# Attention scores in sixteen 32 by 32 tiles instead of four 32 by 128 tiles, and the memory write by the heads of each tile

## The chip, the cores and the metric

One core of one Trainium2 chip. The metric is the time of the kernel on the device in microseconds (us). "Clock" is the mean share of full speed that TensorE (PE) was granted.

## The reference, cut to what matters

Two layers run one after the other, twice, over 2048 tokens of 640 features: an attention with a compressive memory (32 heads of 20 features, four segments of 512 tokens), and a feed-forward block of width 1728. In the attention, every segment `s` does:

```python
logits = jnp.einsum('bhqd,bhkd->bhqk', qs, ks) * scale + mask
p = _softmax(logits, axis=-1)
a_dot = jnp.einsum('bhqk,bhkd->bhqd', p, vs)
# ... read of the memory M, z
o = g * a_mem + (1.0 - g) * a_dot
pk = phi(ks)
M = M + jnp.einsum('bhld,bhle->bhde', pk, vs)
z = z + jnp.einsum('bhld->bhd', pk)
```

The change touches two of these products: the logits (called scores here), and the update of `M`, `z` (the memory write).

## The kernel before

A scheduler written in Python simulates the engines, and fixes the order of every engine's instructions before the program is built. It knows three modes of TensorE: "full" (128 by 128), "cols" (four column tiles of 128 by 32) and "rows" (four row tiles of 32 by 128), and charges 96 ns for a change of mode. A dense product may run in full or in column mode; it takes the mode that TensorE is in, and full mode after scores:

```python
def _mode(self, op):
    if op.cols is None:
        return op.mode
    return self.mode if self.mode != "rows" else "full"

# in _alts:
if e == "pe" and self._mode(op) != self.mode:
    hold = hold + SWITCH_NS          # 96.0
```

Scores. A head has 20 features, so four heads lie at partitions 0, 32, 64 and 96, and their matmuls run at once in four row tiles, one wave of four. A block of scores is one or two such waves and always 512 columns of streaming, because the causal mask shortens the later key blocks:

```python
ROUNDS = (((0, 0, 0),), ((0, 1, 0), (0, 3, 384)), ((0, 2, 0), (1, 2, 256)),
          ((1, 0, 0),), ((1, 1, 0), (1, 3, 384)))     # (group, key block j, column offset)
...
for y, (z, j, o) in enumerate(parts):
    N = L - 128 * j
    fns.append([(lambda e, ...: e.matmul(
        slot.ap[:, q, o:o + N], sl.ap[32 * hh:32 * hh + DH, z, 0, 128 * j:128 * j + 128],
        sl.ap[32 * hh:32 * hh + DH, z, 1, 128 * j:L]),
        y == len(parts) - 1 and hh % 2 == 1) for hh in (2 * k, 2 * k + 1)])
...
return pe(221.0, fns, ..., mode="rows"), None
```

There are 160 such blocks. After each, ScalarE takes the exponential, and later TensorE multiplies the probabilities with the values in four column tiles ("cols").

Memory write. 128 features of the keys against the values of all heads that they touch (7 or 8 heads of 21 columns); a mask drops later what belongs to other heads. In column mode each column tile holds 32 features:

```python
def mm(e, b, rows, part, c=c, i=i, ...):
    return e.matmul(
        b.ap[rows, CH_OFF[c] - o0:CH_OFF[c + 1] - o0], part,
        VAUG[vx(a, s)][:, i, CH_H0[c]:CH_H1[c], :].rearrange("p h e -> p (h e)"),
        start=st, stop=True, skip_group_check=True)
```

The softmax here doesn't subtract the row's maximum and nothing guards it: scores larger than these inputs give would overflow.

Of the kernel before, what the change touches and what calls it, by code (L numbers as in the profile page):

```python
# [12 lines left out]
DH = 20  # L13
# [96 lines left out]
class Op:  # L110
# [4 lines left out]
    def __init__(self, alts, waits, dma=None, acq=None, urgent=False, take=(), mode="full", lag=0.0, port=False):  # L115
        self.lag = lag
        self.port = port
        self.alts = alts
        self.mode = mode
        self.cols = None  # L120
        self.acq = acq
        self.waits = [t for t in waits if t is not None]
        self.dma = dma
        self.urgent = urgent
        self.take = take
# [44 lines left out]
class Sched:  # L170
# [63 lines left out]
    def _alts(self, op):  # L234
        res = []
        waits = op.waits
        if op.acq is not None:
            s = self._pick(op.acq)
            if s is None:
                return res  # L240
            waits = waits + s.tks
        for k, (e, hold, fns, tail) in enumerate(op.alts):
            m = PE_MARGIN if e == "pe" else 0.0
            if e == "pe" and self._mode(op) != self.mode:
                hold = hold + SWITCH_NS
            start = max([self.at(t) + SEM_NS + m for t in waits], default=0.0)
            start = max(self.free[e], start)
            if e == "dve" and op.port and self.free["pool"] > start:
                hold = max(hold, self.free["pool"] - start + PORT_NS)
            res.append((start + hold, start, k, e))  # L250
        return res
# [100 lines left out]
    return Op([("pe", ns, fns, 190.0)], waits, acq=acq, take=take, mode=mode, lag=lag)  # L352


def either(op, cols):
    op.cols = cols
    return op


def quarters(a):  # L360
# [34 lines left out]
def bass_interleave_layers__memory_aug_infini_attn__dense_activation_relu__prompt_kernel(  # L395
    nc, A_x, A_wq, A_wk, A_wv, A_wo, A_beta, B_x, B_w1, B_w2, out,
):
    with contextlib.ExitStack() as es:
# [463 lines left out]
        def vx(a, s):  # L862

            return 2 if (a, s) == (0, 0) else s % 2
# [195 lines left out]
        def mem_write(a, s):  # L1060
            mg = yield Need("maskg")
            if s < NSEG - 1:
                vt = yield Need("v", a, s)
                upd = []
                lastd = None
                for p, cs in enumerate(PARTS):
                    pht = yield Need("phkT", a, s, p)
                    o0 = CH_OFF[cs[0]]
                    w = CH_OFF[cs[-1] + 1] - o0
                    bk = None  # L1070
                    for i in range(NJ):
                        fns, cols = [], []
                        for c in cs:
                            def mm(e, b, rows, part, c=c, i=i, o0=o0, st=(i == 0 and c == cs[0])):
                                return e.matmul(  # L1075
                                    b.ap[rows, CH_OFF[c] - o0:CH_OFF[c + 1] - o0], part,
                                    VAUG[vx(a, s)][:, i, CH_H0[c]:CH_H1[c], :].rearrange("p h e -> p (h e)"),
                                    start=st, stop=True, skip_group_check=True)
                            end = i == NJ - 1 and c == cs[-1]
                            fns.append((lambda e, b=None, bk=bk, mm=mm, kt=phk[:, c, i, :]: mm(e, b or bk, slice(0, 128), kt), end))  # L1080
                            for y, (rows, part) in enumerate(quarters(phk[:, c, i, :])):
                                cols.append((lambda e, b=None, bk=bk, mm=mm, rows=rows, part=part: mm(e, b or bk, rows, part),
                                             end and y == 3))
                        if i == 0:
                            bk, lastd = yield either(pe(66.0 * len(cs), fns, pht + vt, acq=MISC), cols)
                        else:
                            lastd = yield either(pe(66.0 * len(cs), fns), cols)
                    if s == 0:
                        tu = yield dve(w, 1, lambda e, bk=bk, o0=o0, w=w: e.tensor_copy(
                            M_sb[:, o0:o0 + w], bk.ap[:, 0:w]), [lastd] + S.events.get(("BD", a - 1, NSEG - 2), []))  # L1090
                    else:
                        tu = yield dve(w, 1, lambda e, bk=bk, o0=o0, w=w: e.tensor_tensor(
                            M_sb[:, o0:o0 + w], M_sb[:, o0:o0 + w], bk.ap[:, 0:w], ALU.add),
                            [lastd] + S.events[("BD", a, s - 1)])
                    bk.release(tu)
                    PHK[p].release(lastd)
                    if p == 1:
                        S.set("dm", a, s, tks=[lastd])
                    else:
                        bd = yield Acq([BDS])  # L1100
                    tb = yield dve(w, 1, lambda e, o0=o0, w=w: e.tensor_tensor(
                        BD[:, o0:o0 + w], M_sb[:, o0:o0 + w], maskg[:, o0:o0 + w], ALU.mult), [tu] + mg + bd.tks)
                    upd.append(tb)
                S.set("BD", a, s, tks=upd)
            else:
                S.set("dm", a, s, tks=[])
# [8 lines left out]
        def scores():  # L1115

            pads = {}
            LEND_FROM, LEND_TO = ("stg", 0, 0, 4, 1), ("sc", NSEG * 0 + G // 2 - 1, 4, 1)

            def half(h, slot):  # L1120

                m, u, k = HALVES[h]
                parts = ROUNDS[u]
                pd = []
                for z in {z for z, _, _ in parts}:
                    n = 2 * m + z
                    a, r = divmod(n, NSEG * G)
                    key = ("pad", a) + divmod(r, G) + ()
                    if key not in S.events:
                        return None  # L1130
                    pads[m] = S.events[key][0]
                    pd = pd + S.events[key][1:]
                sl = pads[m]
                fns = []
                for y, (z, j, o) in enumerate(parts):
                    N = L - 128 * j
                    fns.append([(lambda e, z=z, j=j, hh=hh, N=N, o=o, sl=sl, q=hh % 2: e.matmul(  # L1137
                        slot.ap[:, q, o:o + N], sl.ap[32 * hh:32 * hh + DH, z, 0, 128 * j:128 * j + 128],
                        sl.ap[32 * hh:32 * hh + DH, z, 1, 128 * j:L]),
                        y == len(parts) - 1 and hh % 2 == 1) for hh in (2 * k, 2 * k + 1)])  # L1140
                return slot, pd, fns

            h = 0
            while h < len(HALVES):
                took = []

                def ask(h=h):
                    if LEND_FROM in S.events and LEND_TO not in S.events:
                        for sl in LENT:
                            if sl in MISC and sl.free:  # L1150
                                MISC.remove(sl)
                                Z.tks = Z.tks + sl.tks
                                if not any(x in MISC for x in LENT):
                                    SC.append(Z)
                    elif LEND_TO in S.events and Z in SC and Z.free:
                        SC.remove(Z)
                        for sl in LENT:
                            sl.tks = Z.tks
                            MISC.append(sl)
                    ready = sorted((s for s in SC if s.free), key=lambda s: max([S.at(t) for t in s.tks], default=0.0))  # L1160
                    if len(ready) < 2 or h + 1 >= len(HALVES):
                        return None, None
                    a, b = half(h, ready[0]), half(h + 1, ready[1])
                    if a is None or b is None:
                        return None, None
                    took[:] = ready[:2]
                    fns = []
                    for y in range(max(len(a[2]), len(b[2]))):
                        for z in (a, b):
                            fns += z[2][y] if y < len(z[2]) else []  # L1170
                    return pe(221.0, fns, a[1] + b[1] + a[0].tks + b[0].tks, take=[a[0], b[0]], mode="rows"), None
                tks = yield Either(ask)
                for tk, sl in zip(tks, list(took)):
                    m, u, k = HALVES[h]
                    S.set("sc", m, u, k, tks=[sl, tk])
                    if (u, k) == (4, 1):
                        pads[m].release(tk)
                    h += 1
# [380 lines left out]
```

## Time and profile before

| | before |
|---|---|
| time, median of 2 runs | 559.84 us (558.76 to 560.91) |
| span of the profiled run | 558.0 us, clock 1.00 |
| score matmuls | 1024 in 160 blocks |
| changes of tile shape on TensorE | 339, together 38.5 us of delay |

The prediction below shows the lines that tell what bounds the kernel. Two more are needed for comparison: the groups of the scores on the profile page (columns: line, engine, operation, names, shapes, count; busy us and mean ns of one; idle time of the engine just before them and who ended most of it).

```profile
L1137 PE MATMUL ps<-pad 20*128 20x512 bf16 (+3 forms) x1024 | 63.4, 301 | 1.7 <-DMA pad<-scr 1.0
L1137 PEld LDWEIGHTS ps<-pad 20*128 20x128 bf16 x1024 | 17.8, 92 | 52.5 <-ACT PT L1199 27.9
```

"20*128" is the tile: 20 rows, 128 weight columns. TensorE hardly idles before scores (1.7 us in all). The idle time of the weight loads, 52.5 us, is no idle time of TensorE: in this trace a load starts 134 ns before its matmul (median) where the shape of the tiles stays, but only 4 ns before it where the shape changes, so its engine shows a gap while matmuls still stream.

### The profile page before, as it was taken

How to read it: one execution, taken by the hardware profiler on the slowest of the kernel's cores; microseconds unless marked ns; L12 is line 12 of the kernel's file. 1: busy time of each engine (PE TensorE's matmuls, PEld its weight loads, DVE VectorE, ACT ScalarE, POOL GpSimd, SP SyncE). 2: the span in 40 equal slices, each digit the busy share in tenths (PEclk: the TensorE clock that was granted, in tenths of full speed). 3: DMA queues.
4: the chain of work that ended last, by engine and by line, in shares of the span. 5: the costliest groups of instructions: out<-in, count | busy, mean ns of one | idle time of the engine just before them, and what ended most of it. 6: DMA issues, size and time to landing. Idle time of an engine off the chain costs nothing.

```text
span 558.0 us, 18924 instructions
## 1 busy us (share of the span) xinstructions
PE 548.0 (98%) x8257; PEld 307.8 (55%) x8257; DVE 422.1 (76%) x1077; ACT 400.1 (72%) x499; POOL 193.5 (35%) x302
## 2 busy tenths in 40 slices
PE   8998999999999999999999999999999999999998
PEld 7454554445554555545446545664545654766756
DVE  5967989979999998797777998688987896552102
ACT  5699888888677987787888887369788678223140
POOL 5336344433344444443433443034334343101000
PEclk9999999999999999999999999999999999999999
DMA  8696999855464417356179231772337511434101
GB/s 271 142 226 156 221 192 207 229 72 110 85 152 83 86 30 173 83 71 113 40 166 168 38 67 41 141 177 46 56 82 176 123 33 20 102 64 47 54 2 51
DMA packets 130005, 61.32 MB, mean 110 GB/s; under 512 B 108802, under 2 KB 119810, under 8 KB 129922
## 3 DMA queue, kind: packets, MB, share of 16 engines
q1 hardware_dynamic: 129504, 59.62, 50.0%
q8 instruction: 65, 1.06, 0.8%
q10 hardware_dynamic: 418, 0.49, 0.3%
q14 instruction: 18, 0.15, 0.1%
HBM read 20.57 MB, written 12.85 MB: 60 GB/s over the span
## 4 chain that ended last, share of the span: by engine, by line
PE 89%; DVE 5%; DMA 4%; SPq 1%; ACT 1%; POOL 0%; issue 0%; ACTq 0%; POOLq 0%
PE ps L636 43%; PE ps L639 26%; PE ps L1137 8%; PE ps L1231 6%; DMA otk<-otu 2%; PE ps L1075 1%; PE ps L1018 1%; PE ps L1270 1%; PE ps L616 1%; PE ps L1411 1%; DMA phk<-phs 1%; DVE stats L657 1%; DVE o_sb L1325 1%; ACT PT L1199 1%; DVE hT L1438 1%; DMA pad<-scr 1%
## 5 line engine op out<-in xcount | busy, mean ns | idle before, releaser
L1199 ACT ACTIVATE PT<-ps 128x1024 bf16<-128x1024 f32 x320 | 309.1, 1026 | 65.8 <-PE ps L1137 63.6
L1211 POOL TENSOR_SCALAR_AFFINE_SELECT PT<-PT 128x512 bf16<-128x512 bf16 x256 | 167.7, 672 | 260.4 <-ACT PT L1199 260.3
L1353 DVE TENSOR_TENSOR x_sb<-x_sb,ps 128x320 bf16<-128x320 bf16 x128 | 60.8, 482 | 68.2 <-PE ps L639 56.0
L636 PE MATMUL ps<-w_r,hT 128*128 128x320 bf16 x470 | 75.1, 300 | 0.0
L636 PE MATMUL ps<-xnT,w_r 128*128 128x512 bf16 x276 | 68.6, 380 | 0.0
L1137 PE MATMUL ps<-pad 20*128 20x512 bf16 (+3 forms) x1024 | 63.4, 301 | 1.7 <-DMA pad<-scr 1.0
L639 PE MATMUL ps<-xnT,w_r 128*32 128x512 bf16 x976 | 59.4, 379 | 0.6 <-DVE hT L1438 0.3
L657 DVE BATCH_NORM_STATS2 stats<-x_sb 128x6 f32<-128x320 bf16 x124 | 55.5, 473 | 3.0 <-DMA x_sb<-in_A_x_dram 2.5
L636 PEld LDWEIGHTS ps<-w_r,hT 128*128 128x128 bf16 x470 | 43.6, 98 | 22.4 <-issue 5.7
L639 PE MATMUL ps<-w_r,hT 128*32 128x320 bf16 x1448 | 55.3, 299 | 0.0
L1137 PEld LDWEIGHTS ps<-pad 20*128 20x128 bf16 x1024 | 17.8, 92 | 52.5 <-ACT PT L1199 27.9
L1438 DVE TENSOR_SCALAR hT<-ps 128x512 bf16<-128x512 f32 x57 | 38.9, 685 | 6.8 <-PE ps L636 5.9
L639 PEld LDWEIGHTS ps<-w_r,hT 128*32 128x32 bf16 x1448 | 37.7, 97 | 11.1 <-DVE x_sb L1353 0.3
L1440 ACT ACTIVATE hT<-ps 128x512 bf16<-128x512 f32 x47 | 28.1, 599 | 20.2 <-PE ps L639 19.2
L1231 PE MATMUL ps<-PT,v_aug 128*21 128x128 bf16 (+3 forms) x896 | 40.4, 301 | 0.0
L636 PEld LDWEIGHTS ps<-xnT,w_r 128*128 128x128 bf16 x276 | 24.6, 97 | 28.2 <-issue 4.8
L1241 DVE CAST otu<-ps 128x512 bf16<-128x512 f32 x47 | 32.1, 684 | 8.6 <-PE ps L1231 8.5
L983 ACT ACTIVATE stg<-stg 128x512 bf16<-128x512 bf16 x50 | 31.4, 633 | 9.8 <-DVE rtmp L981 9.7
L639 PEld LDWEIGHTS ps<-xnT,w_r 128*32 128x32 bf16 x976 | 25.1, 97 | 21.9 <-DVE hT L1438 0.5
L673 POOL TENSOR_TENSOR rstd<-lnU,mhalf 128x2 f32<-128x2 f32 (+2 forms) x26 | 20.7, 796 | 46.1 <-DVE lnU L669 36.8
L636 PE MATMUL ps<-wv_r,xnT 128*128 128x320 bf16 x180 | 33.9, 300 | 0.0
L834 DVE CAST stg<-ps 128x512 bf16<-128x512 f32 x42 | 28.6, 684 | 6.2 <-PE ps L636 5.6
(108 smaller groups left out, 726.1 us busy)
## 6 DMA issues: line engine op xcount, KB each, us to landing
pad<-scr SPq DMA_DIRECT2D x124, 80.0 KB
scr<-stg SPq DMA_DIRECT2D x34, 256.0 KB, 3.3
out_dram<-x_sb SPq DMA_DIRECT2D x16, 160.0 KB, 2.4
w_r<-in_B_w_dram SPq DMA_DIRECT2D x10, 216.0 KB, 2.6
w_r<-in_B_w_dram SPq DMA_DIRECT2D x13, 160.0 KB, 2.8
x_sb<-in_A_x_dram SPq DMA_DIRECT2D x10, 160.0 KB, 3.3
scr<-w_r SPq DMA_DIRECT2D x5, 256.0 KB, 2.8
wv_r<-in_A_wv_dram SPq DMA_DIRECT2D x1, 800.0 KB, 9.0
```

Source lines behind the costliest of these rows:

```text
L636: return e.matmul(view(dst.ap, b), a, b, start=(k == 0), stop=(k == last))
L639: return e.matmul(view(dst.ap[rows], b), part, b, start=(k == 0), stop=(k == last))
L657: tk = yield dve(320, 1, lambda e, c2=c2: e.bn_stats(stats6[:, t % 12, c2, :], x_sb[:, t, c2 * 320:(c2 + 1) * 320]), xt)
L834: te = yield evac(N, 1, lambda e, sg=sg, bk=bk: e.tensor_copy(sg.ap[:, t0:t0 + N], bk.ap[:, 0:N]), lambda e, sg=sg, bk=bk: e.activation(sg ...
L983: te = yield act(512, lambda e, q=q: e.activation(q, q, ACT.Exp), [tr] + p, psum=False)
L1137: fns.append([(lambda e, z=z, j=j, hh=hh, N=N, o=o, sl=sl, q=hh % 2: e.matmul(slot.ap[:, q, o:o + N], sl.ap[32 * hh:32 * hh + DH, z, 0, 12 ...
L1199: tx = yield act(1024, lambda e, dst=dst, src=src: e.activation(dst, src, ACT.Exp, scale=SCALE), sc + pw)
L1211: tm = yield pool(600.0, lambda e, reg=reg: e.affine_select(out=reg, in_=reg, pattern=[[0, 4], [1, 128]], compare_op=ALU.is_ge, fill=0.0, ...
L1231: fns.append((lambda e, OD, j=j, hh=hh: e.matmul(OD.ap[32 * hh:32 * hh + DH + 1, 128 * j:L], VAUG[vx(a, s)][:, j, 4 * g + hh, :], pt.ap[:, ...
L1241: te = yield evac(L, 1, lambda e: e.tensor_copy(dst, OD.ap), lambda e: e.activation(dst, OD.ap, ACT.Copy), [tk] + OTU[0].tks)
L1353: ta = yield dve(320, 1, lambda e: e.tensor_tensor(x_sb[:, t, 320 * hf:320 * hf + 320], x_sb[:, t, 320 * hf:320 * hf + 320], bk.ap[:, 0:32 ...
L1438: th = yield evac(512, 1, lambda e, dc=dc, bk=bk: e.tensor_scalar(hT[:, dc, :], bk.ap[:, :], 0.0, None, ALU.max), lambda e, dc=dc, bk=bk: ...
```

## The change

The idea: neighbours of the scores run in four column tiles, so if the scores too are cut over four column tiles (the 128 keys of a block in four quarters), the two kinds of work share the column cut and might follow one another without a pause. The memory write, in column mode, then streams for each tile only the two or three heads that its 32 features belong to (42 or 63 columns instead of 147), apart from the first token block, which must write the whole width once; the scheduler is told 38 ns for such a group.

```diff
-def either(op, cols):
+def either(op, cols, ns=None):
     op.cols = cols
+    op.cols_ns = ns
     return op
+
+def heads_of(c, q):
+    f = 128 * c + 32 * q
+    return f // DH, (f + 31) // DH + 1
 ...
+            if op.cols_ns is not None and self._mode(op) == "cols":
+                hold = op.cols_ns
 ... memory write:
                             for y, (rows, part) in enumerate(quarters(phk[:, c, i, :])):
-                                cols.append((lambda e, ...: mm(e, b or bk, rows, part),
-                                             end and y == 3))
+                                hs = heads_of(c, y) if i else (CH_H0[c], CH_H1[c])
+                                cols.append((lambda e, ..., hs=hs: mm(
+                                    e, b or bk, rows, part, hs), end and y == 3))
 ...
-                            lastd = yield either(pe(66.0 * len(cs), fns), cols)
+                            lastd = yield either(pe(66.0 * len(cs), fns), cols, 38.0 * len(cs))
 ... scores:
-                    fns.append([(lambda e, z=z, j=j, hh=hh, N=N, o=o, sl=sl, q=hh % 2: e.matmul(
-                        slot.ap[:, q, o:o + N], sl.ap[32 * hh:32 * hh + DH, z, 0, 128 * j:128 * j + 128],
+                    fns.append([(lambda e, z=z, j=j, hh=hh, N=N, o=o, sl=sl, q=hh % 2, c=c: e.matmul(
+                        slot.ap[32 * c:32 * c + 32, q, o:o + N],
+                        sl.ap[32 * hh:32 * hh + DH, z, 0, 128 * j + 32 * c:128 * j + 32 * c + 32],
                         sl.ap[32 * hh:32 * hh + DH, z, 1, 128 * j:L]),
-                        y == len(parts) - 1 and hh % 2 == 1) for hh in (2 * k, 2 * k + 1)])
+                        y == len(parts) - 1 and hh % 2 == 1 and c == 3) for hh in (2 * k, 2 * k + 1) for c in range(4)])
```

The scheduler's modes and its price for a change of mode stay as they were.

## The prediction

> **What bounds the kernel now.** I first read the busy times of the profile page, to see which engine has no slack.
>
> ```profile
> span 558.0 us, 18924 instructions
> PE 548.0 (98%) x8257; PEld 307.8 (55%) x8257; DVE 422.1 (76%) x1077; ACT 400.1 (72%) x499; POOL 193.5 (35%) x302
> ```
>
> TensorE (PE) has work in flight for 98% of the span; VectorE and ScalarE have a quarter of the span free. That alone isn't proof, since the ends of matmuls are modelled and overlap, so I read the chain of waits followed back from the last instruction next.
>
> ```profile
> PE 89%; DVE 5%; DMA 4%; SPq 1%; ACT 1%; POOL 0%; issue 0%; ACTq 0%; POOLq 0%
> PE ps L636 43%; PE ps L639 26%; PE ps L1137 8%; PE ps L1231 6%; DMA otk<-otu 2%; PE ps L1075 1%; PE ps L1018 1%; PE ps L1270 1%; PE ps L616 1%; PE ps L1411 1%; DMA phk<-phs 1%; DVE stats L657 1%; DVE o_sb L1325 1%; ACT PT L1199 1%; DVE hT L1438 1%; DMA pad<-scr 1%
> ```
>
> 89% of the chain is TensorE: L636 and L639 are the dense products in full mode and in four column tiles, L1137 the scores, L1231 the products of probabilities and values. So nearly every nanosecond that the change adds to TensorE's stream, or takes from it, reaches the end. The windows of the scores' line show where they lie (columns: stretch, its length, busy time and count of matmuls and of weight loads, granted clock, DMA).
>
> ```profile
> 0.00:60.00 60.00, 7.92 (x128) 2.23 (x128) 1.00 0.77 201
> 60.00:200.00 140.00, 19.00 (x308) 5.34 (x308) 1.00 0.65 137
> 200.00:350.00 150.00, 20.60 (x332) 5.79 (x332) 1.00 0.47 91
> 350.00:490.00 140.00, 15.84 (x256) 4.45 (x256) 1.00 0.45 95
> ```
>
> All 1024 matmuls of the scores lie before 490 us at full clock; over the same windows all of TensorE is busy 139.43 of 140, 149.03 of 150 and 138.89 of 140 us. There is no idle stretch in which a longer score block could hide.
>
> What does a score block cost? Busy sums don't tell, because four tiles run at once and a record lasts longer than the streaming (mean 385 ns for 512 columns). Starts tell. The timeline of TensorE around one block:
>
> ```profile
> 250.61 0.40 PE L1137 MATMUL ps<-pad 20*128 20x384 bf16 x8
> 250.94 0.72 PE L1231 MATMUL ps<-PT,v_aug 128*21 128x512 bf16 x16
> 251.49 0.60 PE L639 MATMUL ps<-xnT,w_r 128*32 128x512 bf16 x8
> 251.92 0.69 PE L1075 MATMUL ps<-v_aug,phk 128*32 128x147 bf16 x32
> 252.44 0.82 PE L639 MATMUL ps<-xnT,w_r 128*32 128x512 bf16 x12
> 253.19 0.40 PE L1137 MATMUL ps<-pad 20*128 20x256 bf16 x8
> 253.52 0.58 PE L636 MATMUL ps<-wo_r,oT 128*128 128x320 bf16 x3
> ```
>
> From the first score matmul to the next kind of work is 0.33 us, in both blocks shown, for 512 columns of streaming in two waves of four tiles, 213 ns at 2.4 columns a nanosecond (dense groups of 512 columns follow one another every 215 to 216 ns in this trace, so 2.4 is the rate). I took the starts of single records over all 160 blocks: a block of one wave of 512 takes 327 ns, a block of two waves (384 and 128, or 256 and 256) 330 ns, as medians. The excess of 114 to 117 ns is the start spread of four tiles, 10 ns (about 3.3 ns from tile to tile), plus about 104 ns before the next mode's first matmul; the second wave adds only 3 ns. On the way in, 99 ns pass after the streaming of whatever came before.
>
> The excess appears wherever the shape of the tiles changes, summed over the trace: scores to full 123 times, to columns 37; full to scores 105, columns to scores 55; full to columns 19; in all 38.5 us of 558. Without a change dense groups lose 2 to 3 ns. That sum is what I think the change is after.
>
> **What the Trainium skill says.** "TensorEngine Tiling (Array Packing)", section Key Properties: "Changing tiling mode (not just tile) drains the TensorE". The trace agrees, and says more: a change of the rows alone (128x128 to 32x128) costs 98 to 99 ns, a change of the columns alone (128x128 to 128x32) 96 ns, a change of both (32x128 to 128x32) 100 ns. "TensorE: Matmul & The Clock Gate", section Measured speedup vs the span model, gives the span of packed tiles as one matmul plus about 4 ns for every further tile, and has 16 tiles fit it; the trace has 3.3 ns for the four tiles of a score wave and no case of 16. The same page, Architectural detail, gives TensorE a queue of 64 instructions; one wave of sixteen tiles is 32 (a load and a matmul each), a two-wave block exactly 64. No record here shows the queue.
>
> **The change part by part.** First, the scores. Each 32-row tile with 128 weight columns becomes four tiles with 32. The streaming doesn't shrink: four column tiles each pass the same 512 columns at once, as one wide tile did. There are 4096 score matmuls instead of 1024, so TensorE issues 11230 matmuls instead of 8257. Program order tells what the scheduler made of it: it still treats scores as a mode of their own, with the same assumed cost of a switch, and puts nearly the same work next to them. Scores enter from full mode 107 times (105 before) and from columns 53 (55), leave to full 124 (123) and to columns 36 (37); 338 changes in all against 339. So no switch goes away by order, only if the hardware takes 32x32 to 128x32 without a drain. That pair differs in the rows alone, like 128x128 to 32x128, which drains now. I choose: it still costs about 100 ns. Saving 0.
>
> The cost is the start spread. Fifteen steps of 3.3 ns are 50 ns instead of 10: 40 ns later for the last tile, which the next mode has to wait for. Over 160 blocks: 160 x 40 ns = 6.4 us. Then the second wave. In the trace it begins 3 ns after the last tile of the first wave has streamed, so it doesn't follow tile by tile; with sixteen tiles it can spread anew by up to 40 ns more, in the 96 blocks that have one: 0 to 3.8 us. With four tiles this second spread cost almost nothing, so I take a third, 1.3 us. I add 1.7 us, a judgement and not a measurement, for twice or four times the instructions having to get through the sequencer behind a wait: the fastest pair of waves in this trace (84 columns, 8 instructions each) runs at 36 to 40 ns a wave, under 5 ns an instruction, while 32 instructions at that speed would take 150 ns. Sum 9.4 us.
>
> Second, the memory write. In column mode each tile now streams only its two or three heads, 42 or 63 columns, instead of all 147, except for the first token block, which must still write the whole width. Before, 200 of these matmuls ran in column mode, 50 waves of four, at 64 to 65 ns. In the new order there are 7 full-width waves and 39 short ones; by width a short one is 63 / 2.4 + 3 = 29 ns, by the fastest wave seen up to 38. Before 50 x 64 = 3.2 us; after 7 x 65 + 39 x 33 = 1.7 us, plus four more matmuls in full mode at 64 ns, 0.3 us. Saving 1.2 us.
>
> The rest of the reordering moves dense groups between full and column mode at equal streaming and counts as 0. Later score ends delay ScalarE's exponentials by some 40 ns a block; it has 158 us free, so this counts as 0. Net +8.2 us on the stream. Since a few blocks wait for ScalarE anyway (entry from columns means 121 ns against a median of 99, 1.2 us over 55), I pass on some 7.5 us: 559.8 + 7.5 = 567.3, put at 567.5 us.
>
> **The rivals.** (a) Tiles of 32x32 and 128x32 share the column cut, and TensorE drains only when that cut changes. Then 36 + 53 = 89 changes become free, 8.9 us; with the costs above the kernel ends at about 558.5 us. For it speaks that the change seems written for it; against it that the row change alone costs 98 ns with the columns uncut. I give it one in five. (b) Issue becomes the bound: if a pair of load and matmul takes 9.5 ns, as the 38 ns for four would have it, sixteen take 152 ns. One-wave blocks (64) grow by about 133 ns, blocks of 384 and 128 (64) by 112, blocks of two 256 (32) by 166: 21 us, less 1.2, so about 580 us. For it: three fifths of the blocks put 64 instructions in a row, and no trace here shows such a run of short ones. Against it: 12 score instructions start within 25 ns in the block at 250.61. One in four, in a milder form more often. (c) The queue and the pull-ahead of loads hide the spread, tile following tile also across the waves; then the scores cost some 4 us and the time is about 563 us. (d) Every change between scores and other work gets cheap, which would save over 20 us and end under 545; nothing in the trace supports it.
>
> **How the range follows.** The middle is 567.5. The low end, 557, is (a) with little spread; the high end, 582, is (b) nearly in full. Faster by over 2% would need less than 548.6, which only (d) reaches: 0.05. Slower by over 2% starts at 571.0, only 3.5 us above my middle, 22 ns a block, and the uncertain terms (second wave, issue) mostly push up: 0.38. Within 2%: 0.57.
>
> **What would show it.** Right: the change from scores to columns still costs 90 to 115 ns after the last tile; the first wave's starts spread over some 50 ns; a one-wave block takes about 367 ns and a two-wave block 370 to 405, instead of 327 and 330; the memory write's short waves follow one another in 29 to 38 ns; TensorE stays at 98% and the chain stays TensorE's. Wrong: scores follow column products within about 10 ns of the end of streaming (rival a); starts spread over 100 ns or more (rival b); block length unchanged (rival c); or a long idle before scores waiting on ScalarE, which I counted as nothing.

## The result, and the profile after

| | before | after |
|---|---|---|
| time, median | 559.84 us | 567.07 us (2 runs, 566.84 to 567.30) |
| ratio | | 1.0135, 95% interval 1.0096 to 1.0174 |
| span of the profiled run | 558.0 us | 565.2 us |
| one-wave score block, median | 327 ns | 367 ns |
| two-wave score block, median | 330 ns | 370 ns |

A ratio here, with its interval, is the comparison of fast runs with the fast runs of the kernel before in the same rounds. It isn't quite the ratio of the medians, nor that of the means of the runs listed (1.0129 here; the two differ by up to 0.0006). Times of blocks are from the starts of single records: the first score matmul to the first matmul of the next kind.

The busy times and the chain of waits of the changed kernel, from its profile page:

```profile
span 565.2 us, 24861 instructions
PE 553.8 (98%) x11230; PEld 318.8 (56%) x11230; DVE 416.8 (74%) x1063; ACT 406.9 (72%) x513; POOL 192.1 (34%) x302
```

```profile
PE 85%; DMA 6%; DVE 5%; ACT 2%; SPq 1%; issue 1%; POOL 0%
```

TensorE still bounds the kernel: 98% busy, and 85% of the chain. The groups of the scores:

```profile
L1147 PE MATMUL ps<-pad 20*32 20x512 bf16 (+3 forms) x4096 | 70.4, 301 | 3.0 <-issue 1.2
...
L1147 PEld LDWEIGHTS ps<-pad 20*32 20x32 bf16 x4096 | 27.7, 87 | 54.8 <-ACT PT L1210 31.4
```

Four times the matmuls, each as long as before (301 ns on average), and together 7.0 us more of busy time, 70.4 against 63.4. The timeline of TensorE around a score block:

```profile
253.08 0.44 PE L1147 MATMUL ps<-pad 20*32 20x384 bf16 x32
253.45 0.73 PE L1242 MATMUL ps<-PT,v_aug 128*21 128x512 bf16 x16
254.00 0.34 PE L1084 MATMUL ps<-v_aug,phk 128*32 128x42 bf16 x24
254.16 1.48 PE L648 MATMUL ps<-xnT,w_r 128*32 128x512 bf16 x24
```

From the start of the scores to the start of the column products it is 0.37 us here and was 0.33 at 250.61 us of the kernel before, though the two now share the column cut. The 24 short matmuls of the memory write, six waves, take 0.16 us, 27 ns a wave; before, 32 matmuls in eight waves took 0.52 us (251.92 to 252.44), 65 ns a wave.

To see where the 7.2 us of span come from I took, for each wave of matmuls, its start minus the start of the wave before and minus that one's columns at 2.4 a nanosecond, and added these excesses by kind:

| us | before | after | difference |
|---|---|---|---|
| streaming, all columns at 2.4 a ns | 491.0 | 490.1 | -0.9 |
| excess on leaving a score block (160) | 18.5 | 24.5 | +6.0 |
| excess on entering one | 18.1 | 18.5 | +0.4 |
| excess inside score blocks | 1.3 | 3.0 | +1.7 |
| all other excess | 24.5 | 24.4 | 0 |

6.0 of the 7.2 us lie at the exits. The 1.7 us inside blocks are two stalls, at 47 and at 104 us (0.74 and 1.01 us from start to start). The timeline of the second (in square brackets: idle time of the engine before the row, and what ended it):

```profile
103.79 0.42 PE L1147 MATMUL ps<-pad 20*32 20x256 bf16 x26
...
104.95 0.29 PE L1147 MATMUL ps<-pad 20*32 20x256 bf16 x6 [0.74 <-issue]
```

26 of the 32 matmuls of a block go out, then 0.74 us pass in which the profile shows nothing that TensorE waited for, then the last six. The profiles of the other kernels with sixteen tiles and the same number of instructions (scores alone, twice, and the scheduler told) have no stall of this size inside a block, so these 1.7 us need not come back in another run. They look like a wait for instructions. Counted along TensorE's recorded instructions (matmuls, loads, semaphore waits), both stalls come after the 192nd or 193rd of a run of 256. And the packets of the instruction queue (q8 on the page, 16 KB each) keep step with TensorE's instructions, one for about 256: 88 packets for 22,595 here, 65 for 16,656 before. "Half columns, sixteen tiles" below comes back to this.

### The profile page after: what moved, and what is told of

It reads as the page before. It is cut to its first block, busy times and chain, and to the rows that moved or that the text cites. A ratio compares the mean times of both kernels' runs of the same rounds, so it can differ in the third digit from the quotient of the medians.

```text
span 565.2 us, 24861 instructions
## 1 busy us (share of the span) xinstructions
PE 553.8 (98%) x11230; PEld 318.8 (56%) x11230; DVE 416.8 (74%) x1063; ACT 406.9 (72%) x513; POOL 192.1 (34%) x302
## 4 chain that ended last, share of the span: by engine, by line
PE 85%; DMA 6%; DVE 5%; ACT 2%; SPq 1%; issue 1%; POOL 0%
PE ps L645 41%; PE ps L648 24%; PE ps L1147 10%; PE ps L1242 6%; PE ps L1027 1%; DMA pad<-scr 1%; DMA scr<-stg 1%; PE ps L1084 1%; DMA phk<-phs 1%; ACT PT L1210 1%; PE ps L1281 1%; PE ps L1422 1%; DMA otk<-otu 1%; DMA x_sb<-in_A_x_dram 1%; DVE xn_tok L712 1%
## 5 line engine op out<-in xcount | busy, mean ns | idle before, releaser
L645 PE MATMUL ps<-w_r,hT 128*128 128x320 bf16 x511 | 82.2, 300 | 0.0
L1147 PE MATMUL ps<-pad 20*32 20x512 bf16 (+3 forms) x4096 | 70.4, 301 | 3.0 <-issue 1.2
L645 PE MATMUL ps<-xnT,w_r 128*128 128x512 bf16 x262 | 65.7, 380 | 0.0
L648 PE MATMUL ps<-xnT,w_r 128*32 128x512 bf16 x1032 | 62.8, 379 | 0.4 <-DVE hT L1449 0.3
L645 PEld LDWEIGHTS ps<-w_r,hT 128*128 128x128 bf16 x511 | 47.6, 98 | 23.7 <-issue 6.2
L1147 PEld LDWEIGHTS ps<-pad 20*32 20x32 bf16 x4096 | 27.7, 87 | 54.8 <-ACT PT L1210 31.4
L648 PE MATMUL ps<-w_r,hT 128*32 128x320 bf16 x1284 | 49.3, 299 | 0.0
L648 PEld LDWEIGHTS ps<-w_r,hT 128*32 128x32 bf16 x1284 | 33.7, 97 | 9.6 <-DVE x_sb L1364 0.3
L843 DVE CAST stg<-ps 128x512 bf16<-128x512 f32 x39 | 26.6, 685 | 8.3 <-PE ps L645 7.9
L645 PE MATMUL ps<-wo_r,oT 128*128 128x320 bf16 x202 | 32.3, 300 | 0.2 <-DVE x_sb L1364 0.2
```

Source lines behind the costliest of these rows:

```text
L645: return e.matmul(view(dst.ap, b), a, b, start=(k == 0), stop=(k == last))
L648: return e.matmul(view(dst.ap[rows], b), part, b, start=(k == 0), stop=(k == last))
L1147: fns.append([(lambda e, z=z, j=j, hh=hh, N=N, o=o, sl=sl, q=hh % 2, c=c: e.matmul(slot.ap[32 * c:32 * c + 32, q, o:o + N], sl.ap[32 * hh: ...
```

## The experiments

My theory after the result: the sixteen tiles of a block start one after the other, 3.3 ns apart, so the last starts 50 ns after the first instead of 10, and the work behind the block waits for the last; the drain on a change of mode (here: the time from the end of the last tile's streaming to the first start in the next shape) is the same as ever; nothing else matters. Rivals: the other order of work carries the loss; the drain did get cheaper and something else eats it; the issue of instructions is the limit. All runs gave results that passed the comparison with the reference. Five rounds give six runs of the kernel with the profiled one, against eleven of the kernel before.

**Scores alone.** Only the last hunk of the diff; the order of every engine's work is that of the kernel before.

> Only the scores change, to sixteen tiles; every engine's order and the memory write stay exactly as in the kernel before. My theory (the start spread of sixteen tiles, 50 ns instead of 10, delays what follows each of the 160 blocks, once a block, and nothing else changes): blocks of one wave take 367 ns, of two waves 370 ns, against 327 and 330; time +6.0 to +6.8 us, ratio 1.011 to 1.012. Rival 'order' (the loss of the changed kernel comes from its other order of work, not from the tiles): ratio below 1.004. Rival 'fewer drains' (a change between 32x32 and 128x32 tiles costs less): the 37 exits to columns show under 60 ns between the end of the last tile's streaming and the next start, instead of some 91, and the ratio is below 1.009.

Measured: 569.43 us median (566.82 to 572.04) against 559.66; ratio 1.0167, interval 1.0136 to 1.0199. Blocks 367 and 370 ns, as expected. The 37 exits to column work leave 91 ns between the end of the last tile's streaming and the next start, as in the kernel before. One block on the timeline, 0.37 us to the next kind:

```profile
251.47 0.44 PE L1137 MATMUL ps<-pad 20*32 20x384 bf16 x32
251.84 0.82 PE L636 MATMUL ps<-xnT,w_r 128*128 128x512 bf16 x3
```

Repeated later on another chip, beside another experiment:

> The sixteen-tile scores alone once more, unchanged, on the same chip and in the same rounds as the extra wave, since the two differ by under 1%. Both theories expect 1.0167 within its interval, 1.0136 to 1.0199; 'length' expects the extra wave within 0.3% of it, 'instructions' expects it 0.4% or more above.

Measured: 567.77 us median (566.87 to 571.53) against 560.18; ratio 1.0139, interval 1.0112 to 1.0166. So "order" falls: the tiles alone, in the old order, cost what the whole change cost, or more. "Fewer drains" falls by the 91 ns. But the total is 7.8 to 9.3 us, more than the 6.4 us of 160 blocks times 40 ns.

**Memory write alone.** The whole diff but for the scores, so the order of the changed kernel with four row tiles.

> Only the memory write changes (by the heads of each tile, with its shorter time told to the scheduler); scores stay in four row tiles. The order of work is that of the changed kernel. Theory: 7.2 us slower than the changed kernel's scores would make it minus 6.4 us of spread, so about 0 to -1.2 us against the kernel before: ratio 0.998 to 1.001; short waves 25 to 29 ns apart. Rival 'order': ratio near 1.010, since the order is the changed kernel's.

Measured: 558.33 us median (557.56 to 559.26); ratio 0.9968, interval 0.9944 to 0.9991. Short waves 27 ns apart as a median (25 to 33). It is slightly faster than both kernels, and a little better than expected (0.998 to 1.001); the new order costs nothing.

**Order alone.** As the last, but with the memory write at full width:

```diff
-                                hs = heads_of(c, y) if i else (CH_H0[c], CH_H1[c])
+                                hs = (CH_H0[c], CH_H1[c])
```

> The order of work of the changed kernel (scheduler told 38 ns for a short group) but the memory write at full width in every wave and scores in four row tiles. Theory: the narrowing itself is worth 39 waves x (65 - 28) ns = 1.4 us, so this is 1.4 us slower than the kernel with the memory write alone: ratio to before 1.000 to 1.003. Rival 'order': ratio about 1.010 or more.

Measured: 559.72 us; ratio 0.9984, interval 0.9958 to 1.0010. The ratio lies slightly below the expected 1.000 to 1.003, which its interval reaches. The order alone makes no difference that can be told. The narrowing is worth 1.0016 to one, about 0.9 us by the ratios and 1.4 us by the medians; the two intervals overlap, so the size rests on the waves' spacing (39 waves, 37 ns each, 1.4 us).

**Eight tiles.** The dose between 4 and 16:

```diff
-                        slot.ap[:, q, o:o + N], sl.ap[32 * hh:32 * hh + DH, z, 0, 128 * j:128 * j + 128],
+                        slot.ap[64 * c:64 * c + 64, q, o:o + N],
+                        sl.ap[32 * hh:32 * hh + DH, z, 0, 128 * j + 64 * c:128 * j + 64 * c + 64],
```

(for `c` in 0, 1)

> Scores in eight tiles of 32 rows by 64 columns (two column tiles a row tile), all else as before, same order. Theory, a spread of 3.3 ns a tile: last tile starts 23 ns after the first instead of 10, blocks 340 and 343 ns, +2.1 us, ratio 1.0035 to 1.004. Rival 'column cut' (the cost comes with any cut of the columns, for instance by a slower weight load, not with the number of tiles): the same +6.4 us as with sixteen. Rival 'issue' (cost grows faster than the number of tiles once the queue is full): under 1 us here.

Measured: 564.46 us; ratio 1.0077, interval 1.0053 to 1.0101. Blocks of 354 and 357 ns: my 340 and 343 missed by 14 ns, and the time with them (160 x 27 ns are 4.3 us, as measured). It lies between my theory and "column cut". The starts did spread by 23 ns as expected. TensorE's timeline of a one-wave block in this run, 0.35 us to the next kind:

```profile
251.40 0.42 PE L1137 MATMUL ps<-pad 20*64 20x512 bf16 x8
251.75 2.55 PE L636 MATMUL ps<-xnT,w_r 128*128 128x512 bf16 x11
```

The 14 ns show in three places: the second wave's first tile started 27 ns after the end of the streaming of the first wave's first tile, where with four and with sixteen tiles it is 13; the weight loads' records last 102 ns on average, against 92 (128 columns) and 87 (32 columns); those of the matmuls of 512 columns 398, against 385. So the width of the weights has a part of its own: 64 columns at 2.4 a nanosecond are 27 ns, 32 are 13. Where the shape stays, a load starts long before its matmul (134 ns, see above) and can hide under the matmuls before; behind a drain it starts 4 ns before it, so I take its time as exposed. For 128 columns the same 13 ns fit only if they load four times as fast. The Trainium skill names a candidate: "TensorEngine Tiling (Array Packing)", section Restrictions (under Tile-to-Partition Mapping), says that column tiling disables the fast weight load. Then the four row tiles could use it, and the eight and sixteen tiles couldn't. No run here switches it alone, so this reading is argued and not shown. It gives a sum for a block: 3.3 ns for each further tile, plus the load of one tile's weights, plus 213 ns, plus 91 ns of drain. Four tiles: 10 + 13 + 213 + 91 = 327. Sixteen: 50 + 13 + 213 + 91 = 367. Eight of 64 columns: 23 + 27 + 213 + 91 = 354. A second wave adds 3.

**Eight narrow tiles.** A test of that sum by a case that it had not been made from. The result is wrong on purpose (half of the keys get no scores; it still passed the comparison, whose tolerance doesn't notice, so passing isn't proof of a right result here).

```diff
-                        ... and c == 3) for hh in (2 * k, 2 * k + 1) for c in range(4)])
+                        ... and c == 1) for hh in (2 * k, 2 * k + 1) for c in range(2)])
+        # once, at the start: VectorE writes zeros to the score banks
```

> Wrong result on purpose: of the sixteen 32x32 tiles only those of the first two column tiles are computed, so eight tiles of 32 columns (the rest of the score banks is zeroed once at the start, and the scores borrow no third pair of banks, so the order differs: only block lengths are read, no time). It separates the number of tiles from the width of the weights, which the eight-tile run mixed. Theory: a block of one wave is 213 ns of streaming, 3.3 ns for each further tile, the exposed load of one tile's weights (13 ns for 32 columns, 27 ns for 64, at 2.4 columns a ns), and 91 ns of drain: 23 + 13 + 213 + 91 = 340 ns; the second wave's first tile starts 13 ns after the streaming of the first wave's first tile. Rival 'eight tiles are special': 354 ns and 27 ns, as in the run with eight tiles of 64 columns.

Measured (one look, state unknown, clock 0.982, no time read): blocks 340 and 343 ns, second wave 13 ns after the first tile. On the timeline, a one-wave block takes 0.34 us:

```profile
255.17 0.41 PE L1137 MATMUL ps<-pad 20*32 20x512 bf16 x8
255.51 0.82 PE L636 MATMUL ps<-xnT,w_r 128*128 128x512 bf16 x3
```

The sum holds to the nanosecond. The cost of a tile and the cost of wide weights are separate. Where in a block the 13 ns lie stays open: in the run with an extra wave (below) the block lengths fit the sum, but the second wave starts 2 ns after the streaming of the first wave's first tile, and the 13 ns come behind it.

**Half columns, sixteen tiles.** Every score matmul cut into two of half the columns, to see how near the issue limit the sixteen tiles run.

```diff
+                    for x in range(2):
+                        w = N // 2
+                        ...  slot.ap[32 * c:32 * c + 32, q, o + x * w:o + x * w + w], ...
```

> Sixteen tiles, and every score matmul cut into two of half the columns: 64 instructions in a one-wave block (two waves of 256) and 128 in a two-wave block. Same order otherwise, right result. Theory 'queue': TensorE has 64 instructions at hand when the wait ends, later ones come at some 8 ns each (the spacing of the weight loads right behind a score block in the changed kernel): blocks of 64 instructions stay near 371 ns, blocks of 128 end some 64 x 8.3 = 530 ns after their start plus 27 to 53 ns of streaming and 91 ns of drain, 630 to 680 ns; 96 of these add 25 to 30 us to the 16-tile kernel, about 595 to 600 us. Rival 'spread only': issue keeps 3.3 ns a tile throughout, blocks of 128 take 380 to 400 ns, and the time is about 570 to 572 us.

Measured (one round, two runs): 604.32 us; ratio 1.0799, interval 1.0754 to 1.0844. Blocks with 64 instructions take 370 ns, blocks with 128 take 661 to 664 ns. The timeline shows one of each, followed by the next kind:

```profile
253.24 0.73 PE L1139 MATMUL ps<-pad 20*32 20x128 bf16 x64
253.90 0.58 PE L636 MATMUL ps<-w_r,hT 128*128 128x320 bf16 x3
...
256.08 0.44 PE L1139 MATMUL ps<-pad 20*32 20x256 bf16 x32
256.45 0.31 PE L636 MATMUL ps<-w_r,hT 128*128 128x320 bf16 x1
```

0.66 us against 0.37 for the same 512 columns. "Queue" is right in that 64 instructions come at the array's pace and further ones don't, but not in how. The first 64 (32 loads, 32 matmuls) have started after 143 ns in blocks of 192 and 64 columns and after 117 ns in blocks of 128; then come some 135 ns without a matmul; then a load and a matmul start every 8.3 ns, the sixteen of a wave within 125 ns. So 8.3 ns is the pace of a pair and not, as I had expected, of one instruction, and that 661 to 664 ns fell into the expected 630 to 680 is partly luck: the pause fills what the faster pace saves. Why there is a pause no run tells.

The time lies above the expected 595 to 600 us. The longer blocks are worth 28 us by their medians; on top the profile has twelve pauses of 0.36 to 2.3 us, 10.5 us from start to start, for which it names no wait. All but one come after 192 to 194 instructions of a run of 256, like the two stalls of the changed kernel. Like these they end 1.2 to 1.7 us after an instruction packet landed, with as many packets landed as full runs of 256 gone by. In none of the twelve profiles does a matmul past such a place start within 1.2 us of the landing of that packet. The smallest distance was 1.9 us in the kernel before, 2.4 with the extra wave (below), and 1.4 in the changed kernel and with the scores alone. So a late instruction packet is the likely cause of these pauses and of the two stalls; no run changed the packets alone, so it isn't shown.

The two-wave blocks of the changed kernel have exactly 64. Behind them the slower pace begins to show: right behind the block at 253.08 us the first nine instructions (loads and matmuls) of the next products start 1 to 4 ns apart, the three weight loads after them 8 to 9 ns apart, the pace of a pair; behind the block at 250.61 us of the kernel before, the same twelve all start 1 to 4 ns apart.

**Half columns, four tiles.**

> The same cut into half columns with the four row tiles of before: 16 and 32 instructions a block, under the queue's 64. Both theories: each further wave costs only about 3 ns, blocks of one wave 330 ns, of two waves 336 ns; time within 1 us of the kernel before (ratio 0.999 to 1.003). If this is slower by more than 2 us, the cost of cutting is in each matmul and not in the number of instructions in a row.

Measured (one round, two runs, 562.65 and 565.12 us, the second at clock 0.997): ratio 1.0076, interval 1.0032 to 1.0120. Blocks 330 and 335 ns, as expected; these are worth 160 blocks, 64 by 3 and 96 by 5 ns, 0.7 us. The time missed: some 4 us more than before. The profile, of the slower run, has most of it in one place:

```profile
94.16 0.40 PE L639 MATMUL ps<-xnT,w_r 128*32 128x512 bf16 x4 [1.90 <-issue]
...
95.57 3.61 PE L639 MATMUL ps<-xnT,w_r 128*32 128x512 bf16 x36
```

TensorE idles for 1.90 us with no wait that the profile shows (0.27 us at the same line, at 91.8 us, in the kernel before), and behind it the granted clock was 0.56 from 95.5 to 99.0 us: eight groups of 512 columns follow one another after 427 ns instead of 216. Together that is some 3.3 us, and no cost of each matmul. The other run, at clock 1.00, has no profile. The eight-tile run has as many matmuls (9281) and cost no more than its blocks (160 x 27 ns = 4.3 us, measured 4.3), so the bare number isn't it.

**The scheduler told the true length.** The changed kernel with `pe(261.0, ...)` for a score block in place of `pe(221.0, ...)`.

> The changed kernel with the scheduler told 261 ns for a score block instead of 221 (40 ns more, the measured growth), so that it plans the rest around the true length. Block lengths must stay 367 and 370 ns. If the part of the loss above 6.4 us comes from waits that a plan with too short score blocks runs into, this is 1 to 3 us faster than the changed kernel (ratio to before 1.009 to 1.012); if those waits are chance, it lies between 1.011 and 1.018.

Measured: 570.35 us median (569.20 to 573.27); ratio 1.0194, interval 1.0162 to 1.0226. Blocks 367 and 370 ns again. By its ratio it is slower than both expectations, though the interval reaches into the second, and against 2% it is unclear; it isn't faster. So a plan with the true length didn't recover the waits. It isn't a clean test: the new plan also differs elsewhere (16 waves of the memory write in column mode instead of 46).

**An extra wave.** What do longer blocks cost by themselves? The kernel before with 88 columns of each block computed twice:

```diff
+                    for N, last in ((88, False), (N, True)) if y == 0 else ((N, True),):
                         fns.append([... e.matmul(slot.ap[:, q, o:o + N], ...,
-                        sl.ap[32 * hh:32 * hh + DH, z, 1, 128 * j:L]), ...
+                        sl.ap[32 * hh:32 * hh + DH, z, 1, 128 * j:128 * j + N]), ...
```

> The kernel before, four row tiles, but each score block first computes 88 of its columns once more (four more matmuls; the same values written twice). Blocks should take 367 ns (one wave) and 370 ns (two waves), the lengths that the sixteen tiles have, with 8 more instructions a block instead of 24 or 48. Theory 'length': the sixteen tiles cost what the longer blocks cost, the 6.4 us themselves and the waits that come of a program order fixed for shorter blocks, so this is as slow as the scores alone in sixteen tiles: +8 to +10 us, ratio 1.014 to 1.018. Theory 'instructions': the 2 to 3 us above 6.4 come from the number of instructions: +6 to +7 us, ratio 1.010 to 1.0125.

Measured: 565.35 us median (564.53 to 566.37); ratio 1.0086, interval 1.0064 to 1.0108. Blocks 366 and 369 ns; one on the timeline, 0.36 us:

```profile
251.94 0.43 PE L1138 MATMUL ps<-pad 20*128 20x88 bf16 x8
252.30 2.55 PE L636 MATMUL ps<-xnT,w_r 128*128 128x512 bf16 x11
```

The scores in sixteen tiles, in the same rounds, had 1.0139 (1.0112 to 1.0166). So blocks as long as theirs, made with four tiles, cost 4.8 us (3.6 to 6.0 by the interval), not 6.4: by this difference 1.6 us of the longer blocks fell into waits that were there anyway. In the profiled runs it is less, 0.3 us: the spans differ by 5.9 us, the blocks by 6.2. And the sixteen tiles cost 3.0 us more than their length explains (by the ratios; 2.4 by the medians). "Length" alone falls; "instructions" is right about the gap between the two, but put this kernel too high (1.010 to 1.0125). Instruction traffic grew by over a third; the pages' rows of the instruction queue (packets, MB, share of the engines' span), before and for the scores again:

```profile
q8 instruction: 65, 1.06, 0.8%
```

```profile
q8 instruction: 89, 1.46, 1.1%
```

The last packet before each of the two stalls of the changed kernel had landed 0.8 and 0.7 us before the stall began; none was under way during it.

Where do the 3 us arise? I took the steps from wave to wave that were over 0.1 us longer than is usual between the same two shapes. What they are longer by adds up, in single profiles, to 8.7 us before, 8.0 with the extra wave, and 12.7 and 10.8 in the two runs of the scores alone. The extra wave and the scores beside it differ by 2.8 us there and by 2.8 us in their spans (563.9 and 566.7 us), so in these profiles the gap lies in waits. About half of it recurs at two places in both runs of the scores alone. One is before the column products at 109.9 and 109.4 us; here for the second run, then for the extra wave:

```profile
109.42 0.72 PE L1232 MATMUL ps<-PT,v_aug 128*21 128x512 bf16 x16 [1.15 <-DVE hT L1439]
```

```profile
108.09 0.72 PE L1232 MATMUL ps<-PT,v_aug 128*21 128x512 bf16 x16 [0.19 <-DVE hT L1439]
```

VectorE was late because it had itself waited for a transfer (otk<-otu), 1.73 and 1.23 us in the two runs and 0.64 with the extra wave. The other place is before dense products at 62.2 and 61.2 us (0.47 and 0.48 us, behind VectorE's rden; no such wait with the extra wave). Why sixteen tiles make these late isn't settled.

## Why the prediction was right, point by point

The time, 567.07 us, fell 0.4 us from the predicted 567.5. The sum under it was right in its large term and in its signs; two small terms were wrong in kind. That the errors cancelled to 0.4 us is luck: the second wave's 1.3 us were nothing, two stalls stood in for the issue term, and by the interval of two runs the loss is only known to be 5.4 to 9.7 us.

- *A change between 32x32 and 128x32 still drains: saving 0.* Right, and shown: 91 ns after the last tile with four tiles, with sixteen, and in the scores alone. This was the choice that mattered most. It came from the trace of before, where a change of the rows alone cost 98 ns with the columns uncut.
- *Start spread, 40 ns a block, 6.4 us.* Right: spreads of 50 and 10 ns, blocks of 367 and 327 ns, and the same steps at eight tiles once the width of the weights is taken apart.
- *Second wave, 1.3 us.* Wrong. I had read from four tiles that the second wave waits for the last tile of the first, because it began 3 ns after that one's end. With sixteen tiles it begins 37 ns before that, and 13 ns after the end of the first tile, as with four: the waves follow tile by tile. I read the 13 ns as the exposed weight load of the first wave; that with four tiles the spread is 10 and 10 + 3 = 13 was chance. The two-wave blocks grew by 40 ns like the others, so this term is 0.
- *Issue, 1.7 us by judgement.* The size came near to what the runs leave over (1.4 to 3 us above 6.4), but not at the place given. Up to 64 instructions in a row a block is no longer than the start spread makes it. What is left lies in waits for other engines, and in the profile of the changed kernel in two stalls that look like late instruction packets. The waves of 84 columns that this term was weighed against show no issue pace: 84 columns stream for 35 of their 36 to 40 ns.
- *Memory write, 1.2 us saved.* Right: waves of 27 to 28 ns, 0.9 us less streaming, ratio 0.9968 for that part with its order.
- *Some 0.7 us absorbed.* Of the right kind, the size open: the extra wave shows 1.6 of 6.4 us by its ratio, 0.3 of 6.2 in its profile.
- Rival (a), no drain between tiles with the same column cut: not so. Rival (b), issue as the bound: not so at 64 instructions, and nearly so beyond: its pair of load and matmul took 9.5 ns, half columns showed 8.3 (blocks of 661 to 664 ns, and 604 us for the kernel). Rival (c), spread hidden: true across the two waves, not at the exit. Rival (d): nothing of it.

A version that beats both kernels came out by the way: the memory write alone, 558.33 us, 0.3% under the kernel before (interval 0.1 to 0.6%).

## What to carry to other kernels

Cutting a matmul that already streamed at full width into more tiles didn't shorten it here; it bought a longer start spread, paid at each exit to another tile shape (40 ns). It could have paid back only by removing a drain, which the shared column cut didn't do. Before writing such a change, take from the trace what a change of the rows alone and of the columns alone costs now. And count instructions in a row between two changes of shape: here a block of 64 ran at the array's pace, and twice as many made it 80% longer.

## What the Trainium skill lacked or had wrong

- "TensorEngine Tiling (Array Packing)", Key Properties, says that a change of mode drains TensorE, but not for how long, nor whether two shapes with the same row or column cut count as one mode. Here 128x128 to 128x32 costs 96 ns of lost streaming and 128x128 to 32x128 98 to 99 ns; 32x32 to 128x32 leaves 91 ns after the last tile. Rows alone, columns alone and both drain about alike.
- "TensorE: Matmul & The Clock Gate", Measured speedup vs the span model, has about 4 ns a tile. The runs have 3.3 ns at 4, 8 and 16 tiles (10, 23 and 50 ns), paid once per run of waves, not once per wave; the page doesn't treat several waves.
- The same page, section LDWEIGHTS, gives columns divided by 1.2, so 27 ns for 32 and 53 ns for 64. Behind a drain, at full clock, the block lengths fit an exposed load of 13 and 27 ns, half of that, and 13 ns for 128 columns without column tiling. The records of the loads themselves differ by 15 ns (87 and 102), not by 27.
- No page gives what happens behind 64 instructions in a row: here a pause of some 135 ns, then a load and a matmul every 8.3 ns (blocks of 128 instructions 661 to 664 ns, of 64 instructions 370 ns).
- No page gives what a late instruction packet costs a program that runs straight on. The two stalls inside a score block (0.74 and 1.01 us from start to start) and the twelve pauses with half columns (10.5 us) look like that; the profile names no wait for them.
